# First token block in two halves, whole-row loads of q and k for two tiles, and new orders of the queues

## The chip, the cores and the metric

The kernel runs on one core of one Trainium2 chip. The metric is the device time of one execution in microseconds, median of three runs. A profile is one execution in the hardware profiler, with times counted from its first instruction. Engines are named as the profile names them: PE multiplies matrices, DVE is the vector engine, ACT the scalar engine, POOL is GpSimd, SP issues the DMAs. PEld is PE's weight load, SPq is SP's queue.

## What is computed

Chunked attention over 64 tokens at a time, then a feed-forward layer with softplus on all 4608 tokens:

```python
B, H, S, D = 8, 8, 576, 64          # chunk = 64, nc = 9
scores = scale * np.matmul(q_c, k_c.transpose(0, 1, 2, 4, 3))
scores = scores - np.max(scores, axis=-1, keepdims=True)
attn = np.exp(scores)
attn = attn / (np.sum(attn, axis=-1, keepdims=True) + 1e-09)
out = np.matmul(attn, v_c)
x = out.transpose(0, 2, 1, 3).reshape(B * S, H * D)      # 4608 x 512
h = x @ w_in                                             # w_in 512 x 2048
g = np.maximum(h, 0.0) + np.log1p(np.exp(-np.abs(h)))
return (g @ w_out).astype(np.float32)                    # w_out 2048 x 512
```

q, k and v are float32; w_in and w_out come as float64, 8 bytes a value.

## The kernel before

**Tiles and blocks.** A tile is 128 tokens (two chunks of 64), 36 in all. Four tiles are a token block m of 512 tokens, nine in all. The hidden width of 2048 is cut in 16 strips of 128. Each of the 144 pairs (m, strip), numbered g, has a first product `gemm1` (12 matmuls of 128x512 into one half of a PSUM tile `pa`), a softplus on ACT (`sp_g`, writes `u`), a split of `u` into a rounded part `g_hi` (ACT, `sp_hi`) and a rest `g_lo` (DVE or POOL, `sp_lo`), and a second product `gemm2` (12 matmuls into four PSUM tiles `po`, one a tile, over all 16 strips). Three matmuls stand for one full product, hi times lo, lo times hi and hi times hi. In PE's order G2 of pair g stands behind G1 of pair g+1: G1_0, G1_1, G2_0, G1_2, G2_1 and so on.

**Attention.** Tiles 0 to 3 go ahead of the first G1, step by step: q and k are loaded as whole rows, transposed by PE (`pe_t`), multiplied (`pe_s`), softmaxed on DVE and ACT, transposed (`pe_e`, then ACT copies), multiplied with v (`pe_v`) and split into x_hi (`att_xh`, ACT) and x_lo (`att_xl`, DVE). From tile 4 on the tiles go in pairs, as bursts of small 64x64 matmuls between the G1 and G2 of certain pairs: S of tiles 4 and 5 behind G1_3; then P V of one pair of tiles together with S of the next two, behind G1_8, behind G1_15, and behind two strips of each later block. For them `blk_load` brings q and k by 8 DMAs of 32 KB each, so placed that one DVE transpose of 128x512 by 32x32 blocks (`blk_t`) gives the operand. After the softmax DVE transposes again (`blk_e`) and 8 DMAs of 32 KB inside the chip (`blk_swap`) exchange quarters of 32 partitions.

**Weights.** 32 units (16 strips of w_in, 16 of w_out) are loaded in 512 KB DMAs (`w_load`, into a ring of three `raw` tiles) and made from float64 into a hi and a lo part: `w_top` (ACT or POOL) and `w_low` (ACT) pick pieces, `w_add` (DVE) joins them, `w_hi` and `w_lo` split the sum. Units go in the order in0, in1, out0, in2, out1, in3, ... and each must be done before its first G1 or G2; after G2_15 no weight is touched again.

**The order.** `Plan` is a list scheduler that runs when the kernel is built: each step is a task with an engine, a cost in us, the tasks it needs and an urgency; `emit` writes the steps in the order in which the plan starts them. On the chip every engine takes its instructions in that order. Tables such as `TOP_ACT`, `HI_POOL`, `LO_POOL` and `GLO_POOL` say which engine does which step. `keep_warm` writes idle matmuls of a 128x128 identity where the plan sees PE wait. All DMAs are issued by SP in one queue, 976 of them. The built program has eight DMA semaphores which take turns: a DMA waits until the one eight places ahead has landed.

Of the kernel before, what the change touches and what calls it, by code (L numbers as in the profile page):

```python
# [33 lines left out]
class Plan:  # L34
# [6 lines left out]
    FLYING = 5  # L41
# [6 lines left out]
    def add(  # L48
        self, name, eng, cost, fn, needs=(), urg=0.0, table=None, take=(), kb=0, slack=0.0, after=(), port=False
    ):  # L50
        self.tasks[name] = dict(
            name=name, eng=eng, cost=cost, fn=fn, needs=list(needs) + list(after), after=set(after), urg=urg, table=table,
            take=take, kb=kb, slack=slack, seq=len(self.tasks), port=port or eng == "POOL",
        )

    def order(self):
# [7 lines left out]
        wait, flying = {}, []  # L64
# [28 lines left out]
        while times:  # L93
# [3 lines left out]
            flying = [e for e in flying if e > now]  # L97
            for eng in list(wait):
                if free.get(eng, 0.0) > now + 1e-9 or eng == "SP" and len(flying) >= self.FLYING:
                    continue  # L100
# [17 lines left out]
                if t["kb"]:
                    dma_free = max(now + 1.8, dma_free) + t["kb"] * 1024 / self.RATE
                    end = max(dma_free + 0.8, end + 2.0)  # L120
                    flying.append(end)
# [21 lines left out]
def chunked_attention_softplus_ffn(  # L143
# [92 lines left out]
    def w_top(u):
        top = tops[u % TOP_BUFS].bitcast(F16).rearrange("p (f t) -> p f t", t=2)[:, :, 1]
# [124 lines left out]
    def pe_e(i):  # L362
        tp = ps_o.tile([P, DM], F32, name="po")
# [73 lines left out]

    def blk_swap(i):
        ea = live.pop(("eA", i))
        eT = blk_tile("eT").rearrange("p (u h k) -> p u h k", u=2, h=H)  # L440
# [5 lines left out]
        live["eT", i] = lambda r, c2, j, h2: eT[r, :, 4 * c2 + 2 * j + h2, :]  # L446
# [35 lines left out]
    def blk_v(i, pa):  # L482
        eT, vt = live.pop(("eT", i)), live.pop(("v", i))
        for j in range(2):
            for c2 in range(2):
                for h2 in range(2):
                    for a in range(2):
# [4 lines left out]
                            pa[o, a, col : col + C], vt[r, 4 * j + 2 * h2 + c2, :], eT(r, c2, j, h2),  # L492
# [79 lines left out]
    def store(m, t):  # L572
# [5 lines left out]
    T0, TG = 18.0, 5.5  # L578
    TK = (0,2)
# [33 lines left out]
    for u, (g, is_in, fc) in enumerate(units):  # L613
# [23 lines left out]
        plan.add(last[0], ph_, 0.65 if ph_ == "POOL" else 0.53, partial(w_hi, u, is_in, fc),  # L637
# [5 lines left out]
    for i in range(FIRST_BLK):  # L643
        d, kw = -60 + 3 * i, KS
        two = 2 * i // NCH != (2 * i + 1) // NCH
        for pl, (n, src) in enumerate((("q", q), ("k", k), ("v", v))):
            plan.add(f"{n}{i}", "SP", 0.6 * (1 + two), partial(pe_load, nc.sync, i, src, pl),
                     urg=VQ + i if pl == 2 else d - 6 + 0.1 * pl, kb=310,
# [145 lines left out]
```

## Time and profile before

| | us |
|---|---|
| device time, median of 3 runs | 885.03 (883.99 to 887.68) |
| the profiled execution, its own time | 883.88 |
| its span, first to last instruction | 882.0 |
| PE busy | 861.7 (98%) |
| DVE, ACT, POOL busy | 329.8, 316.8, 56.1 |
| mean granted TensorE clock | 0.998 |

The profile is read from the top down: the share of each engine, then the waits of PE, then the stretches in which they lie, and last the instructions around each wait with what released them. Matmuls of PE overlap in the records, so a group of 12 with a mean of 390 ns each takes less than 12 times that; the distance from one start to the next is what counts.

### The profile page before, as it was taken

Reading aid. Unit: us, or ns where it says so; the run is one execution under the profiler, and the core shown is the slowest. Engines: PE = TensorE matmul, PEld = TensorE weight load, DVE = VectorE, ACT = ScalarE, POOL = GpSimd, SP = SyncE. Lnnn points to the kernel's source line nnn. Section 1 sums busy time; section 2 is a strip of 40 time slices with the busy share of each in tenths; the row PEclk is TensorE's granted clock in tenths of the full one; section 3 lists DMA queues with packets and bytes.
Section 4 is the critical chain, followed back from the end, with each engine's and each line's share of the span. In section 5 each row is a group of like instructions: output and inputs, shape, how many; then the busy total and the mean of one; then the engine's idle time right before and its main releaser. Section 6 shows DMA issues by size and latency. Waiting matters only on the chain.

```text
span 882.0 us, 14812 instructions
## 1 busy us (share of the span) xinstructions
PE 861.7 (98%) x5868; PEld 700.9 (79%) x5868; DVE 329.8 (37%) x550; ACT 316.8 (36%) x494; POOL 56.1 (6%) x58
## 2 busy tenths in 40 slices
PE   8699989999999999999999999999999999999998
PEld 7577878888888888888888888888888888888886
DVE  5667854333415251524233432334153414121111
ACT  4677763232424242324232422333232423232222
POOL 1353630000000000000000000000000000000000
PEclk9999999999999999999999999999999999999999
DMA  9676763313232324132412232232223231000001
GB/s 224 171 200 201 208 149 92 62 39 63 41 86 40 63 41 100 28 64 41 105 30 46 52 62 74 41 66 42 81 39 63 44 94 31 18 18 31 1 1 48
DMA packets 214852, 63.91 MB, mean 72 GB/s; under 512 B 191744, under 2 KB 208128, under 8 KB 214784
## 3 DMA queue, kind: packets, MB, share of 16 engines
q1 hardware_dynamic: 214784, 62.98, 31.7%
q8 instruction: 46, 0.75, 0.4%
q14 instruction: 22, 0.18, 0.1%
HBM read 45.09 MB, written 9.44 MB: 62 GB/s over the span
## 4 chain that ended last, share of the span: by engine, by line
PE 87%; DMA 6%; SPq 2%; ACT 2%; POOL 1%; issue 1%; DVE 1%; DVEq 0%; ACTq 0%; POOLq 0%
PE po L560 43%; PE pa L527 41%; DMA raw<-in_moe_w_out_dram 3%; PE pa L491 2%; DMA raw<-in_moe_w_in_dram 2%; PE pa L424 2%; SPq L305 1%; DMA q<-in_q_dram 1%; ACT top L239 0%; SPq L228 0%; POOL top L239 0%; ACT low L248 0%; ACT u L538 0%; DMA k<-in_v_dram 0%; DVE low L253 0%
## 5 line engine op out<-in xcount | busy, mean ns | idle before, releaser
L538 ACT ACTIVATE u<-pa 128x512 f32<-128x512 f32 x144 | 86.0, 597 | 498.5 <-PE pa L527 498.4
L546 DVE TENSOR_TENSOR g_lo<-u,g_hi 128x512 fp32r<-128x512 f32 x136 | 94.6, 695 | 356.7 <-ACT g_hi L542 356.3
L527 PE MATMUL pa<-x,wib 128*128 128x512 f32 x864 | 208.7, 390 | 1.9 <-DVE wib L278 1.9
L527 PEld LDWEIGHTS pa<-x,wib 128*128 128x128 f32 x864 | 161.6, 188 | 38.1 <-DVE wib L278 2.3
L527 PE MATMUL pa<-x,wi_hi 128*128 128x512 f32 x576 | 178.0, 390 | 1.4 <-DVE x L507 1.4
L560 PE MATMUL po<-late,g_hi 128*128 128x512 f32 x540 | 172.1, 394 | 0.0
L527 PEld LDWEIGHTS pa<-x,wi_hi 128*128 128x128 f32 x576 | 108.1, 188 | 24.1 <-DVE x L507 1.8
L560 PEld LDWEIGHTS po<-late,g_hi 128*128 128x128 f32 x540 | 101.2, 187 | 24.4
L560 PE MATMUL po<-wo_hi,g_lo 128*128 128x512 f32 x288 | 115.6, 401 | 3.1 <-DVE g_lo L546 3.1
L560 PE MATMUL po<-late,g_lo 128*128 128x512 f32 x288 | 114.6, 398 | 0.0
L560 PE MATMUL po<-wo_lo,g_hi 128*128 128x512 f32 x288 | 114.4, 397 | 0.0
L560 PE MATMUL po<-wo_hi,g_hi 128*128 128x512 f32 x288 | 113.8, 395 | 0.0
L527 PE MATMUL pa<-x,wi_lo 128*128 128x512 f32 x288 | 112.8, 392 | 0.0
L542 ACT CAST g_hi<-u 128x512 fp32r<-128x512 f32 x144 | 89.2, 619 | 4.4
L560 PEld LDWEIGHTS po<-wo_hi,g_lo 128*128 128x128 f32 x288 | 54.4, 189 | 16.5 <-DVE g_lo L546 3.3
L527 PEld LDWEIGHTS pa<-x,wi_lo 128*128 128x128 f32 x288 | 54.0, 188 | 14.1 <-PE po L560 2.8
L560 PEld LDWEIGHTS po<-wo_hi,g_hi 128*128 128x128 f32 x288 | 54.4, 189 | 13.4
L560 PEld LDWEIGHTS po<-wo_lo,g_hi 128*128 128x128 f32 x288 | 54.4, 189 | 12.8
L560 PEld LDWEIGHTS po<-late,g_lo 128*128 128x128 f32 x288 | 54.0, 187 | 13.1
L455 DVE TENSOR_REDUCE mx<-pa 128x8 f32<-128x512 f32 x32 | 22.0, 686 | 70.0 <-ACT x L503 68.5
L412 DVE STREAM_TRANSPOSE ka<-k 128x512 f32<-128x512 f32 x30 | 21.3, 710 | 52.8 <-DMA k<-in_k_dram 42.5
L471 DVE TENSOR_REDUCE den<-qe 128x8 f32<-128x512 f32 x32 | 21.1, 660 | 16.6 <-ACT qe L466 16.6
(97 smaller groups left out, 546.0 us busy)
## 6 DMA issues: line engine op xcount, KB each, us to landing
out_dram<-raw SPq DMA_DIRECT2D x36, 256.0 KB, 2.6
raw<-in_moe_w_in_dram SPq DMA_DIRECT2D x16, 512.0 KB, 4.6
raw<-in_moe_w_out_dram SPq DMA_DIRECT2D x16, 512.0 KB, 4.5
eT<-ka SPq DMA_DIRECT2D x256, 32.0 KB, 1.9
q<-in_q_dram SPq DMA_DIRECT2D x240, 32.0 KB, 2.1
k<-in_k_dram SPq DMA_DIRECT2D x240, 32.0 KB, 2.1
q<-in_v_dram SPq DMA_DIRECT2D x60, 64.0 KB, 2.4
k<-in_v_dram SPq DMA_DIRECT2D x60, 64.0 KB, 2.4
```

The lines of the kernel that those rows point to most:

```text
L305: eng.dma_start(dst[p0 : p0 + rows], src[b, :, s0 : s0 + rows, :].rearrange("h s d -> s h d"))
L412: nc.vector.transpose(t, live.pop((n, i)))
L424: nc.tensor.matmul(pa[o, c2, col : col + C], qT[r, a * HP + hl, :], kT[r, a * HP + hl, :], start=True, stop=True,)
L455: nc.vector.tensor_reduce(mx, sc, axis=AX.X, op=ALU.max)
L471: nc.vector.tensor_reduce(den, e, axis=AX.X, op=ALU.add)
L491: nc.tensor.matmul(pa[o, a, col : col + C], vt[r, 4 * j + 2 * h2 + c2, :], eT(r, c2, j, h2), start=True, stop=True,)
L527: nc.tensor.matmul(ph, wt[:, c, fs], x[:, :, c, :], start=(n == 0), stop=(n == 3 * KC - 1))
L538: nc.scalar.activation(w["u"], w["ph"], AF.Softplus)
L542: nc.scalar.copy(w["hi"], w["u"])
L546: (nc.gpsimd if pool else nc.vector).tensor_tensor(w["lo"], w["u"], w["hi"].bitcast(F32), op=ALU.subtract)
L560: nc.tensor.matmul(pos[w["m"]][t], gg[:, ts_], wt, start=(w["first"] and n == 0), stop=(w["last"] and n == 2),)
```

## The change

It has four parts.

1. **Block 0 in halves.** `HALVES = 1`: the pair g=0 becomes two, `a0` for tiles 0 and 1 and `0` for tiles 2 and 3. Its `gemm1` makes 12 matmuls of 256 columns for each half, its softplus, hi and lo have 256 columns, its `gemm2` 6 matmuls of 512 columns for each. PE's order is G1_a0, G1_0, G2_a0, G1_1, G2_0, G1_2, ..., with the steps of tile 3's attention wherever the plan puts them.
2. **Whole rows.** Tiles 4 and 7 (`WHOLE`) load q and k by whole rows: 1 DMA of 256 KB, or 2 of 128 KB where the tile spans two batches (tile 4). `blk_t4` makes the operand by 8 DVE transposes of 32 partitions each (four for each chunk), in the place of one of 128 partitions.
3. **Tile 7's exchange.** `SWAP_DVE = (7,)`: in the place of `blk_e` and the 8 DMAs of `blk_swap`, `blk_e4` makes 8 DVE transposes of 32 partitions.
4. **Planned anew.** The planner now follows each DMA of a step by itself, with eight in flight (`FLYING = 8`); its costs, urgencies and tables have other numbers, the second burst of each later block moves from strip 13 to 14 (`BURST_AT`), and tile 2's k copy moves from DVE to ACT (`TK`). 942 DMAs are issued instead of 976.

```diff
-    FLYING = 5
+    FLYING = 8
+    AHEAD = 3.2
...
+        if i in WHOLE:
+            for p0, rows, b, s0 in rows_of(i):
+                nc.sync.dma_start(
+                    hd(dst)[p0 : p0 + rows], src[b, :, s0 : s0 + rows, :].rearrange("h s d -> s h d")
+                )
+            return
...
+    def blk_t4(i, n, c2):
+        if c2 == 0:
+            live[n + "T", i] = blk_tile({"q": "qe", "k": "ka"}[n])
+        src, dst = (t.rearrange("p (h a d) -> p h a d", h=H, a=2) for t in (live[n, i], live[n + "T", i]))
+        for tb in range(2):
+            for dh in range(2):
+                d, s = (2 * c2 + dh) * BL, (2 * c2 + tb) * BL
+                nc.vector.transpose(dst[d : d + BL, :, tb], src[s : s + BL, :, dh])
...
+    def blk_e4(i, a):
+        e = live["e", i].rearrange("p a j (u k) -> p u (a j) k", u=2)
...
+        for tb in range(2):
+            for kb in range(2):
+                d, s = (2 * a + kb) * BL, (2 * a + tb) * BL
+                nc.vector.transpose(live["eT", i][d : d + BL, tb], e[s : s + BL, kb])
...
-        ph = pa_tile()[:, 0, :MT]
+        ph = pa_tile()[:, 0, : w["cols"]]
...
-                    ph, wt[:, c, fs], x[:, :, c, :], start=(n == 0), stop=(n == 3 * KC - 1)
+                    ph, wt[:, c, fs], x[:, ts_, c, :], start=(n == 0), stop=(n == 3 * KC - 1)
...
-        for t in range(TPM):
-            ts_ = slice(t * P, (t + 1) * P)
+        for j, t in enumerate(w["tiles"]):
+            ts_ = slice(j * P, (j + 1) * P)
...
-    TOP_ACT = (0,1,4,8,9,10,11,12,13,14,15,16,18,19,23,24,26,28,29,30,31)
+    TOP_ACT = (0,3,8,9,11,15,16,17,20,21,25,26,29)
...
-    BURST_AT = (6, 13)
-    QK_AFTER = "v0"
+    BURST_AT = (6, 14)
+    QK_AFTER = "load1"
...
+    ahead = [dict(w, name=f"a{w['g']}", tiles=range(TPM // 2)) for w in blocks[:HALVES]]
+    for w in blocks[:HALVES]:
+        w["tiles"] = range(TPM // 2, TPM)
...
+            if i in SWAP_DVE:
+                plan.add(f"Tf{i}", "DVE", 1.6, partial(blk_e4, i, 0), [f"norm{i}"] + gone, urg=d)
+                plan.add(f"Te{i}", "DVE", 1.6, partial(blk_e4, i, 1), [f"Tf{i}"], urg=d)
+                swapped[i] = f"Te{i}"
...
+    for n, w in enumerate(ahead + blocks):
+        seq.append(f"G1_{w['name']}")
+        if n >= HALVES:
+            seq += [f"B{w['g']}_{j}" for j in range(2) if w["g"] in bursts]
+        if n >= LAG:
+            seq.append(f"G2_{(ahead + blocks)[n - LAG]['name']}")
```

**The start of block 0, on PE and ACT.** On PE before, the transpose of tile 3's softmax (L366), fillers (L322), its product with v (L382), fillers, and then G1_0 with 512 columns:

```order
L366 MATMUL po<-ident,x 128x128 x4
L322 MATMUL pa<-ident 128x128 x2
L382 MATMUL pa<-x,eT 64x64 x16
L322 MATMUL pa<-ident 128x128 x5
L527 MATMUL pa<-x,wi_lo 128x512
L527 MATMUL pa<-x,wi_hi 128x512 x2
```

On PE now, the last matmuls of G1_a0 (L567, 256 columns), then the same steps of tile 3 (L374, L330, L390), then the first of G1_0:

```order
L567 MATMUL pa<-x,wi_lo 128x256
L567 MATMUL pa<-x,wi_hi 128x256 x2
L374 MATMUL po<-ident,x 128x128 x4
L330 MATMUL pa<-ident 128x128 x2
L390 MATMUL pa<-x,eT 64x64 x16
L330 MATMUL pa<-ident 128x128 x6
L567 MATMUL pa<-x,wi_lo 128x256
```

The half for tiles 0 and 1 moved ahead of tile 3's last steps. On ACT before, from tile 3's x_hi (L503) to the first `g_hi` (L542); L239 is `w_top` of the unit out1, the two L248 are `w_low` of out1 and in3, L538 the load of softplus's table and the first softplus:

```order
L503 CAST x<-pa 128x512
L274 CAST wi_hi<-wib 128x4x128
L239 CAST top_98<-raw 128x512
L248 ACTIVATE wib<-raw 128x512 x2
L538 ACT_TABLE_LOAD
L538 ACTIVATE u<-pa 128x512
L274 CAST wi_hi<-wib 128x4x128
L542 CAST g_hi<-u 128x512
```

On ACT now, from `w_top` of the unit in2 (L247) to the second softplus; L256 are `w_low` of in2, out1 (x2) and in3, L542 is tile 3's x_hi:

```order
L247 CAST top_99<-raw 128x512
L578 ACT_TABLE_LOAD
L578 ACTIVATE u<-pa 128x256
L378 COPY x<-po 128x512
L582 CAST g_hi<-u 128x256
L256 ACTIVATE wib<-raw 128x512 x2
L542 CAST x<-pa 128x512
L282 CAST wi_hi<-wib 128x4x128
L256 ACTIVATE wib<-raw 128x512
L578 ACTIVATE u<-pa 128x256
```

The table load and the first softplus moved ahead of `w_low` of in2, out1 and in3; `w_low` of out1 now stands ahead of tile 3's x_hi.

**SP's queue behind the first loads.** Before, from the load of the unit in1 on; `q` and `k` are tile 4's, `x` is tile 5's q and k:

```order
L228 DMA raw<-in_moe_w_in_dram 128x4x512
L233 DMA raw<-in_moe_w_out_dram 128x2048
L404 DMA q<-in_q_dram 32x8x32 x8
L228 DMA raw<-in_moe_w_in_dram 128x4x512
L404 DMA k<-in_k_dram 32x8x32 x8
L233 DMA raw<-in_moe_w_out_dram 128x2048
L228 DMA raw<-in_moe_w_in_dram 128x4x512
L404 DMA x<-in_q_dram 32x8x32 x8
L233 DMA raw<-in_moe_w_out_dram 128x2048
L404 DMA x<-in_k_dram 32x8x32 x8
```

Now, from the same load on:

```order
L234 DMA raw<-in_moe_w_in_dram 128x4x512
L239 DMA raw<-in_moe_w_out_dram 128x2048
L234 DMA raw<-in_moe_w_in_dram 128x4x512
L408 DMA q<-in_q_dram 64x8x64 x2
L408 DMA k<-in_k_dram 64x8x64 x2
L239 DMA raw<-in_moe_w_out_dram 128x2048
L419 DMA x<-in_q_dram 32x8x32 x8
L234 DMA raw<-in_moe_w_in_dram 128x4x512
L419 DMA x<-in_k_dram 32x8x32 x8
L239 DMA raw<-in_moe_w_out_dram 128x2048
```

in2 moved ahead of tile 4's q, and tile 4's 16 issues became 4. Further on, the load of the last strip of w_in is the 136th DMA of the queue, where it was the 170th.

**DVE before the second burst.** Before, from the transpose of tile 4's softmax (L436) on; `k` is tile 6's, `x` tile 7's, L253 is `w_add`, L278 `w_lo`, L546 `g_lo`:

```order
L436 STREAM_TRANSPOSE ka<-qe 128x512
L412 STREAM_TRANSPOSE qe<-q 128x512
L436 STREAM_TRANSPOSE ka<-qe 128x512
L412 STREAM_TRANSPOSE qe<-x 128x512
L253 ISA wib<-wib,top_98 128x1024
L253 ISA wib<-wib,top_99 128x1024
L546 TENSOR_TENSOR g_lo<-u,g_hi 128x512
L278 TENSOR_TENSOR wi_lo<-wib,wi_hi 128x4x128
L253 ISA wib<-wib,top_98 128x1024
L412 STREAM_TRANSPOSE ka<-k 128x512
```

Now the last third of the stretch ahead of that burst; L426 is `blk_t`, L436 `blk_t4`:

```order
L426 STREAM_TRANSPOSE ka<-k 128x512
L436 STREAM_TRANSPOSE qe<-x 32x8x32 x4
L286 TENSOR_TENSOR wib<-low,wib 128x4x128
L261 ISA low<-low,top_98 128x1024
L261 ISA low<-low,top_99 128x1024
L286 TENSOR_TENSOR wo_lo<-low,wo_hi 128x512
L436 STREAM_TRANSPOSE ka<-x 32x8x32 x4
L586 TENSOR_TENSOR g_lo<-u,g_hi 128x512
L436 STREAM_TRANSPOSE ka<-x 32x8x32 x4
L261 ISA low<-low,top_98 128x1024
```

Tile 7's two transposes became four groups of four, spread between the weights' steps and a `g_lo`.

## Rows read from the trace of the kernel before

**Rows 1.** PE's waits: line, who released it, us in total, times, longest.

```profile
PE po L560 <- DVE g_lo L546: 3.1, 1, 3.1
PE pa L527 <- DVE wib L278: 1.9, 1, 1.9
```

**Rows 2.** Stretch: length, busy us by engine (instructions), PE clock, DMA share, GB/s.

```profile
132.00:820.00 688.00, 687.94 (x4571) 558.28 (x4570) 235.88 (x408) 219.60 (x337) 3.14 (x3) 1.00 0.26 54
```

**Rows 3.** The chain that ended last, 66 to 72 us: start, us, what.

```profile
66.29 2.79 PE po L560 x12
69.09 2.73 PE pa L527 x12
```

**Rows 4.** Timeline of PE, block 0: start, us, instruction, idle before and releaser.

```profile
31.21 0.50 PE L527 MATMUL pa<-x,wi_hi 128*128 128x512 f32 x1 [1.44 <-DVE x L507]
...
36.54 0.60 PE L322 MATMUL po<-ident 128*128 128x128 f32 x4
40.22 0.79 PE L560 MATMUL po<-wo_hi,g_lo 128*128 128x512 f32 x1 [3.08 <-DVE g_lo L546]
...
44.69 0.40 PE L527 MATMUL pa<-x,wi_lo 128*128 128x512 f32 x1
```

**Rows 5.** Timeline of ACT, 33 to 38 us.

```profile
33.04 0.78 ACT L239 CAST top<-raw 128x512 f16<-128x512 bf16 x1 [1.84 <-DMA raw<-in_moe_w_out_dram]
...
35.15 0.67 ACT L248 ACTIVATE wib<-raw 128x512 int32<-128x512 uint32 x1 [0.81 <-DMA raw<-in_moe_w_in_dram]
35.84 1.28 ACT L538 ACT_TABLE_LOAD   x1
37.13 0.60 ACT L538 ACTIVATE u<-pa 128x512 f32<-128x512 f32 x1
```

**Rows 6.** Timeline of DVE, the first lo part.

```profile
39.48 0.69 DVE L546 TENSOR_TENSOR g_lo<-u,g_hi 128x512 fp32r<-128x512 f32 x1 [0.60 <-ACT g_hi L542]
```

**Rows 7.** A stretch with its granted clock; columns as in rows 2.

```profile
41.00:42.00 1.00, 1.00 (x4) 0.80 (x3) 1.00 (x1) 0.51 (x1) 1.00 (x1) 0.50 0.46 92
```

**Rows 8.** Timeline of SP's queue: start, us of issuing, DMAs.

```profile
15.01 1.90 SPq L228 DMA_DIRECT2D raw<-in_moe_w_in_dram  x1
...
17.60 5.15 SPq L404 DMA_DIRECT2D q<-in_q_dram  x8
...
27.51 0.40 SPq L233 DMA_DIRECT2D raw<-in_moe_w_out_dram  x1
...
115.44 0.39 SPq L228 DMA_DIRECT2D raw<-in_moe_w_in_dram  x1
```

**Rows 9.** Groups of instructions: count, busy us, mean ns of one, idle before.

```profile
L412 DVE STREAM_TRANSPOSE ka<-k 128x512 f32<-128x512 f32 x30 | 21.3, 710 | 52.8 <-DMA k<-in_k_dram 42.5 <-DMA eT<-ka 10.2
...
L472 DVE TENSOR_SCALAR den<-den 128x8 f32<-128x8 f32 x36 | 7.5, 210 | 1.2
...
L334 PE MATMUL po<-ident,late 128*128 128x128 f32 x24 | 3.0, 276 | 0.0
```

**Rows 10.** Groups of instructions, PE's weight loads.

```profile
L527 PEld LDWEIGHTS pa<-x,wi_hi 128*128 128x128 f32 x576 | 108.1, 188 | 24.1 <-DVE x L507 1.8
```

**Rows 11.** Timeline of PE: bursts behind G1_3, G1_8, G1_15 and, last, an undisturbed one.

```profile
54.38 0.69 PE L424 MATMUL pa<-ka,qe 64*64 64x64 f32 x32 [0.63 <-ACT u L538]
...
82.78 0.69 PE L491 MATMUL pa<-eT,x 64*64 64x64 f32 x29
...
87.58 0.50 PE L560 MATMUL po<-wo_hi,g_lo 128*128 128x512 f32 x1
...
130.68 0.51 PE L491 MATMUL pa<-eT,k 64*64 64x64 f32 x19 [0.48 <-DMA k<-in_v_dram]
...
170.51 0.69 PE L491 MATMUL pa<-eT,q 64*64 64x64 f32 x32
...
172.56 0.50 PE L560 MATMUL po<-wo_hi,g_lo 128*128 128x512 f32 x1
```

**Rows 12.** Stretch between the first two bursts; columns as in rows 2.

```profile
60.00:85.00 25.00, 23.99 (x164) 19.39 (x162) 19.31 (x27) 18.74 (x31) 12.22 (x11) 1.00 0.69 203
```

More of the change, by code (lines that the diff above doesn't have):

```diff
@@ L48, in add @@
     def add(
-        self, name, eng, cost, fn, needs=(), urg=0.0, table=None, take=(), kb=0, slack=0.0, after=(), port=False
+        self, name, eng, cost, fn, needs=(), urg=0.0, table=None, take=(), kb=0, slack=0.0, after=(), port=False, parts=1
     ):
@@ L63, in order @@
         fin, issued, free, tab, dma_free, port = {}, {}, {}, None, 0.0, 0.0
-        wait, flying = {}, []
+        wait, landed = {}, {}
         times = [0.0]
@@ L114, in order @@
                     end = port = max(now, port) + cost
+                last = end
+                if t["kb"]:
+                    end, lanes = now, landed.setdefault(eng, [0.0] * self.FLYING)
+                    for _ in range(t["parts"]):
+                        end = max(end, lanes[-self.FLYING] + 0.1, dma_free - self.AHEAD) + cost / t["parts"]
+                        dma_free = max(end + 1.0, dma_free) + t["kb"] * 1024 / self.RATE / t["parts"]
+                        lanes.append(max(dma_free + 0.7, end + 1.8))
+                    last = lanes[-1]
                 free[eng] = end
@@ L117, in order @@
                 issued[t["name"]] = end
[L118 to L121, printed above, removed]
+                end = last
                 fin[t["name"]] = end
@@ new lines, in chunked_attention_softplus_ffn @@
+        needs += [f"xl{m * TPM + t}" for t in w["tiles"]]
+        plan.add(f"G1_{name}", "PE", 2.78 if part == 1 else 1.5, partial(gemm1, w), needs, urg=1e6, take=[("pa", [f"sp{name}"])])
+        plan.add(f"sp{name}", "ACT", 0.1 + 0.5 * part, partial(sp_g, w), [f"G1_{name}"], urg=-2, table="softplus",
+                 take=[("u", [f"lo{name}"])], after=[f"exp{FIRST_BLK - 1}"] if SP_EXP and name == "a0" else [])
+        plan.add(f"hi{name}", "ACT", 0.1 + 0.52 * part, partial(sp_hi, w), [f"sp{name}"], urg=-1, take=[("g", [f"G2_{name}"])])
@@ new lines, in chunked_attention_softplus_ffn @@
+        pool = name in GLO_POOL
+        plan.add(f"lo{name}", "POOL" if pool else "DVE", 1.3 if pool else 0.1 + 0.58 * part, partial(sp_lo, w, pool),
+                 [f"hi{name}"], urg=-1)
+        take = [("po", [f"ev{m}_{t}"]) for t in w["tiles"]] if w["first"] else []
+        plan.add(f"G2_{name}", "PE", 2.78 * part, partial(gemm2, w),
+                 [before[f"G2_{name}"], f"lo{name}", f"w_lo{of_out[fc]}", f"w_hi{of_out[fc]}"], urg=1e6, take=take,
+                 after=[f"S{FIRST_BLK - 1}"] if m == 0 and w["first"] else [])
```

143 lines of the change are left out of this document (81 added, 62 removed).

## The prediction, before the changed kernel ran

> **What bounds the kernel.** The page's busy shares say PE, 98%, but an average over the span hides where the rest lies. So the second view is PE's busy time by stretch: from 132 us to 820 us it works 687.94 of 688 us at full clock [rows 2]. Nothing on another engine can shorten that part, and the change removes no matmul from it. In the chain of work a G2 and the next G1 take 2.79 + 2.73 = 5.52 us [rows 3]; that is the dense pitch by which I measure everything ahead of 132 us. The third view is PE's own waits: the longest is the first G2 for `g_lo`, 3.1 us, another is G1_15 for a weight, 1.9 us [rows 1]. The fourth is the timeline around each wait. The time can only come from PE's holes ahead of 132 us, or be lost by new ones.
>
> Hole one is G2_0. G1_1 has issued its last matmul when the fillers start at 36.54; the first G2 starts at 40.22, 3.68 us later [rows 4]. Backwards: `g_lo` started at 39.48 [rows 6], it needed `g_hi`, which needed the softplus at 37.13; that stood behind the table load at 35.84, and this behind a weight's `w_low`, which waited for its DMA until 35.15 [rows 5]. G1_0 had finished issuing at about 33.8 (31.21 + 2.73 less one matmul), so the first softplus waited on ACT for a load it has no use for.
>
> Hole two follows from it: G2_0 takes from 40.22 to 44.69, 4.47 us [rows 4], where 2.79 is dense. [...] That is 1.68 us.
>
> Hole three is the first bursts and G1_15. The burst behind G1_8 takes from 82.78 to 87.58, 4.80 us, where an undisturbed one takes 172.56 - 170.51 = 2.05: 2.75 us lost. The bursts behind G1_3 and G1_15 lost 0.63 and 0.48 [rows 11], G1_15 the 1.9. Together 5.76 us.
>
> **The change, part by part.**
>
> *Halves.* x_lo of tile 3 ended G1_0's wait at 31.21 [rows 4]. The half a0 needs tiles 0 and 1 only, so its matmuls lie ahead of tile 3's last steps, in PE time that was idle or filler. What then remains of G1 0 is half of it, 2.73/2 = 1.37 us less. A matmul of 256 columns is in no row. The nearest are 128x128 transposes, 24 in 3.0 us or 0.125 us each [rows 9], the weight load, 0.188 us [rows 10], and half of the dense 0.2275, 0.114. I take 0.13 (the weight changes with each matmul, as in the transposes): 12 x 0.13 = 1.6 us, 0.23 over the half; bounds 1.37 and 2.26 us. [...] G2 makes the same 12 matmuls in two halves: nothing. Net gain 1.37 - 0.23 = 1.14 us, if the remaining half can start no later than before.
>
> *Can it?* x_hi of tile 3 now stands on ACT behind `w_low` of out1. Before, out1's issue came at 27.51, because tile 4's q held the queue for 5.15 us from 17.60 and its k followed; it landed at 33.04 [rows 5, 8]. Now in2 and four issues lie between: five times about 0.6 us, so the queue is free near 20.6. But out1 also needs in1's `raw` buffer: in1, issued at 15.01, lands near 21 and `w_top` takes 0.78. So the issue comes at about 21.8, 5.7 us earlier, the landing at 33.04 - 5.7 = 27.3 or, as it now follows 1 MB closely, 28.7. Then `w_low` 0.67, x_hi 0.6, a `w_add` 0.65 and x_lo 0.68 on DVE (partly side by side): G1_0's half starts near 31.0. I count no gain and no loss here; bounds -1 (tile 3's own chain) and +4 us (out1 as late as before).
>
> *Softplus.* The table load now follows `w_top` of in2, which lands near 24.5 instead of 27, since it is issued where q was, at 17.60. Table 1.28 and softplus follow G1_a0, and `g_lo` of a0 is there about 2 us ahead of G2_a0, which follows G1_0 at once. `g_lo` of the second half has G2_a0 and the whole G1_1 to hide in, 1.4 + 2.73 us, against a chain of 0.35 + 0.35 + 0.4 plus a wait for in3's `w_low`, some 2 us. So hole one closes, 3.68 us (bounds 0 and 3.68). With no stretch of 3 us without work ahead of the first G2, hole two closes too: 1.68 us. The cover would be gone if in3 lands over 2 us later than I think.
>
> *The queue of loads.* 34 DMAs fewer are issued, and the last strip of w_in is the 136th instead of the 170th. Between 27.51 (the 33rd) and 115.44 (the 170th) one issue took (115.44 - 27.51)/137 = 0.64 us [rows 8]. The last strip so comes about 34 x 0.64 = 22 us earlier by count; in part the queue will wait for buffers and for the swaps of tiles 4 and 5, which must follow their softmax, so I take 13. The demand comes 8 to 9 us earlier (3.68 + 1.68 + 1.14 = 6.5 from the start, the rest from the first bursts). G1_15's 1.9 us and the 0.48 go. The burst behind G1_8 needs the last DMA of v of tile 5, now 27 places earlier (17 us), but those DMAs follow the swap of tile 5, which moves with the first burst, 6.5 us. I leave it 1.2 us of its 2.75, the first burst 0.3, and 0.5 for waits that I don't see: 5.76 - 2.0 = 3.8 us gained; bounds 5.8 (none left) and -3.
>
> *DVE transposes.* Tiles 4 and 7 trade five transposes of 0.71 us [rows 9] for 40 of 32 partitions and 256 elements each. No row has one. A 128x8 operation takes 0.21 and the 128x512 transpose 0.71 [rows 9]; between them by elements, 0.45. So 40 x 0.45 - 3.6 = 14 us more DVE work. Between 60 and 85 us DVE is busy 19.31 of 25 us [rows 12], and tile 7's 16 lie in that stretch: 16 x 0.45 - 1.4 = 5.8 us. It becomes full and just not late; queued behind them are `g_lo` and `w_add`, and PE waits for those. Bounds: 0.21 and 0.71 each. [...] Hidden, I count nothing.
>
> *The rest.* The later bursts move one strip back; in rows 2 they cost no wait, and three products lie between x_lo and its first use. POOL gets more weight steps; its 12.22 of 25 us [rows 12] has room. Moving tile 2's copy to ACT: inside the lead.
>
> **Sum.** 3.68 + 1.68 + 1.14 + 3.8 = 10.3 us. The profiled execution took 883.88, so 873.6; the median lies 1.15 above that execution, so 874.7.
>
> **Rivals.**
> *A, out1 late.* If it lands near 33 as before, x_lo of tile 3 comes at 35 and G1_0's half with it: 4 us back, about 879. For it: 1 MB in flight ahead of it. Against: the queue ahead of it is 7 us shorter (10 less 3).
> *B, DVE full.* At 0.71 us a piece, tile 7's 16 take 4 us more, and the burst behind G1_8 or a `g_lo` waits: about 879.
> *C, the loads set the pace.* The holes at 82 and 125 us show weights and v arriving just when PE wants them. If they come no earlier, PE starts 6.5 us earlier only to wait: 883, no change. Against: 34 issues fewer.
> *D, slower.* A small transpose costs over twice a whole one, as its source and target partitions differ and no row shows that. Tile 7's q and k are needed behind G1_8, where my walk leaves 3 us to spare: 16 x (t - 0.45) - 3 exceeds the gain of 10.3 from t = 1.28 us on, and 10.3 + 4.4 (0.5% slower) from 1.56 on; at 1.8 it gives 893. Against: 0.71 for twice the elements.
>
> **Chances.** Forecast 0.62, A 0.12, B 0.12, C 0.09, D 0.05. Within 0.5% (about what a measurement here can tell from no change) is 880.6 to 889.5. A and B lie below it: faster 0.85, same 0.10, slower 0.05. The range takes the forecast's bounds and A and B: low 870 (no later wait, tile 3 one microsecond earlier), high 881.
>
> **What would show it.** PE's waits should no longer list the first G2 for `g_lo`; the clock should stay at 1.00 from 30 to 50 us; G1_2 should start near 38.2 instead of 44.69; `w_low` of out1 on ACT should end its wait near 29; the 32-partition transposes should take about 0.45 us, the 256-column matmuls 0.13 in pitch. I am wrong if ACT waits for a load between G1_a0 and the first `g_hi`, if PE waits for `g_lo` or tile 7's operands near 76 us, or if PE's holes ahead of 132 us stay near 13 us in all.

## The result, and the profile after

The changed kernel takes 878.05 us (median of 4, 877.37 to 878.49); the kernel before 886.22 beside it. The ratio is 0.9909, 95% interval 0.9884 to 0.9935: faster by 0.9%, as predicted, but by less than predicted (874.7 was 10.3 us under the 885.03 of before). The profiled execution took 878.49 us with a span of 876.7, against 883.88 and 882.0: these 5.3 us of span are what the traces can explain. The medians lie 8.2 us apart. The profiled execution of before lies below the four timed ones (883.99 to 887.68), and the longer executions of that kernel have a lower mean granted clock (beside e9 and e10 a span of 886.6 us at 0.990, 881.4 at 0.998); no profile shows where they lose it, so the other 3 us stay open. Of all executions behind this text one, of e3, was slow (1423.12 us at a granted clock of 0.557) and is left out of e3's median and ratio. From 132 to 820 us PE works 687.94 us in both [rows 2], so the gain lies ahead of 132 us. In starts (us) read from PE's timelines:

| | G1_2 | G1_4 | G1_9 | G2 behind the burst of G1_15 | span |
|---|---|---|---|---|---|
| before | 44.69 | 57.88 | 90.48 | 131.65 | 882.0 |
| after | 43.12 | 55.94 | 88.06 | 126.32 | 876.7 |
| gained | 1.57 | 1.94 | 2.42 | 5.33 | 5.3 |

So the later holes gave 5.3 - 1.57 = 3.7 us, where the sum had 3.8. The head gave 1.57 instead of 6.5. PE's waits of after (columns as in rows 1); the first G2 and G1_15 are gone from the list, the wait for `x_lo` of tile 3 (1.44 before, rows 4) is now the longest, and v is waited for behind G1_8:

```profile
PE pa L567 <- DVE x L546: 2.1, 1, 2.1
PE po L374 <- DVE late L517: 2.1, 3, 1.2
...
PE pa L530 <- DMA x<-in_v_dram: 1.2, 2, 0.6
```

PE's timeline of after, against rows 4 and 11:

```profile
32.18 0.39 PE L567 MATMUL pa<-x,wi_lo 128*128 128x256 f32 x1 [0.27 <-ACT x L542]
34.67 0.67 PE L567 MATMUL pa<-x,wi_hi 128*128 128x256 f32 x2 [2.10 <-DVE x L546]
...
37.06 0.63 PE L600 MATMUL po<-wo_hi,g_lo 128*128 128x512 f32 x1
...
43.12 0.40 PE L567 MATMUL pa<-x,wi_lo 128*128 128x512 f32 x1
...
84.20 0.51 PE L530 MATMUL pa<-eT,x 64*64 64x64 f32 x19 [0.59 <-DMA x<-in_v_dram]
...
85.17 0.50 PE L600 MATMUL po<-wo_hi,g_lo 128*128 128x512 f32 x1
```

The half of G1_0 starts at 32.18, stops after one matmul for `x_lo` of tile 3 and goes on at 34.67; I had said 31.0. From there to G1_1 at 38.99 it takes 4.32 us for 11 matmuls of 256 columns (1.3 at the pitch below) and half a G2 (1.40). The stretches (columns as in rows 2) show why: the granted clock is at 0.50 again from 36 to 38 us, as it was in hole two (rows 7), and costs 1.6 us (4.32 less 1.3 and 1.40), as before.

```profile
34.00:36.00 2.00, 1.33 (x7) 1.33 (x8) 1.99 (x5) 0.00 (x0) 0.61 (x1) 0.71 1.04 276
36.00:38.00 2.00, 2.00 (x9) 1.81 (x9) 1.93 (x5) 1.35 (x3) 0.77 (x1) 0.50 0.50 76
```

VectorE's timeline says what `x_lo` stood behind:

```profile
27.18 1.29 DVE L261 CUSTOM_DVE_ANT_0 wib<-wib,top 128x1024 uint16<-128x1024 uint16 x1
...
29.00 1.77 DVE L436 STREAM_TRANSPOSE qe<-q 32x256 f32<-32x256 f32 x4
30.80 0.43 DVE L586 TENSOR_TENSOR g_lo<-u,g_hi 128x256 fp32r<-128x256 f32 x1
31.14 2.88 DVE L261 CUSTOM_DVE_ANT_0 wib<-wib,top 128x1024 uint16<-128x1024 uint16 x2
33.94 0.68 DVE L546 TENSOR_TENSOR x<-pa,x 128x512 fp32r<-128x512 f32 x1
```

Its `x_hi` ended on ACT at 32.13, but VectorE's queue held two `w_add`s until 33.94. The engine had no room: from 24 to 50 us VectorE was busy 14.45 of 26 us in the kernel before (first line) and 25.36 in the changed one (second):

```profile
24.00:50.00 26.00, 20.05 (x147) 16.21 (x147) 14.45 (x23) 15.81 (x26) 9.62 (x10) 0.93 0.76 186
```

```profile
24.00:50.00 26.00, 21.41 (x162) 18.07 (x163) 25.36 (x44) 15.78 (x28) 13.13 (x14) 0.93 0.75 184
```

And there is a view of before that I had read only for its pitch [rows 3]: the chain that ended last, here from 16 to 56 us: its shares and three of its pieces (start, us, what).

```profile
by line: DMA raw<-in_moe_w_in_dram 39.4%; DMA raw<-in_moe_w_out_dram 21.5%; DMA q<-in_q_dram 12.4%; POOL top L239 5.4%; SPq L228 4.8%; ACT top L239 3.9%; PE po L560 2.8%; issue 2.7%; DVE wib L253 2.2%; PE pa L424 1.7%; ACT u L538 1.5%; ACT 
...
28.02 7.11 DMA raw<-in_moe_w_in_dram
...
46.37 4.51 DMA raw<-in_moe_w_in_dram
...
53.73 0.60 ACT u L538
```

It runs through the loads to the softplus ahead of the first burst, and not through holes one and two at all. In the changed kernel the same view from 23 to 36 us runs through VectorE (first line: `w_add`, the small transposes, `x_lo`):

```profile
by line: DVE wib L261 35.9%; DVE qe L436 12.7%; issue 12.7%; PE pa L567 11.7%; DVE x L546 10.3%; DVE mx L494 5.3%; DVE den L510 4.7%; DVE wi_lo L286 4.6%; DVE g_lo L586 3.3%; DVE den L512 1.6%; DVE den L511 1.4%; DVE x L499 0.3%
```

### The profile page after: what moved, and what is told of

It reads as the page before. It is cut to its first block, busy times and chain, and to the rows that moved or that the text cites. A ratio compares the mean times of both kernels' runs of the same rounds, so it can differ in the third digit from the quotient of the medians.

```text
span 876.7 us, 14820 instructions
## 1 busy us (share of the span) xinstructions
PE 861.6 (98%) x5874; PEld 701.5 (80%) x5874; DVE 348.5 (40%) x589; ACT 309.4 (35%) x483; POOL 65.3 (7%) x68
## 4 chain that ended last, share of the span: by engine, by line
PE 89%; DMA 4%; DVE 4%; SPq 1%; issue 1%; ACT 1%; POOL 0%; DVEq 0%; POOLq 0%; ACTq 0%
PE po L600 42%; PE pa L567 41%; PE pa L530 2%; DMA raw<-in_moe_w_in_dram 2%; PE pa L449 2%; DMA raw<-in_moe_w_out_dram 1%; PE po L330 1%; DVE wib L261 1%; SPq L322 1%; DVE mx L494 0%; DVE den L510 0%; DMA q<-in_q_dram 0%; DMA x<-in_v_dram 0%; DVE g_lo L586 0%; DVE x L546 0%
## 5 line engine op out<-in xcount | busy, mean ns | idle before, releaser
L578 ACT ACTIVATE u<-pa 128x512 f32<-128x512 f32 (+1 forms) x145 | 86.2, 594 | 510.1 <-PE pa L567 505.4
L586 DVE TENSOR_TENSOR g_lo<-u,g_hi 128x512 fp32r<-128x512 f32 (+1 forms) x137 | 94.9, 693 | 295.3 <-ACT g_hi L582 295.0
L567 PE MATMUL pa<-x,wib 128*128 128x512 f32 x864 | 208.6, 390 | 0.0
L567 PEld LDWEIGHTS pa<-x,wib 128*128 128x128 f32 x864 | 161.7, 188 | 36.0 <-PE po L600 2.4
L567 PE MATMUL pa<-x,wi_hi 128*128 128x512 f32 (+1 forms) x584 | 179.3, 389 | 2.1 <-DVE x L546 2.1
L567 PEld LDWEIGHTS pa<-x,wi_hi 128*128 128x128 f32 x584 | 109.9, 189 | 24.3 <-DVE x L546 2.3
L567 PE MATMUL pa<-x,wi_lo 128*128 128x512 f32 (+1 forms) x292 | 114.0, 390 | 1.3 <-POOL top L247 1.0
L582 ACT CAST g_hi<-u 128x512 fp32r<-128x512 f32 (+1 forms) x145 | 89.4, 616 | 4.4
L567 PEld LDWEIGHTS pa<-x,wi_lo 128*128 128x128 f32 x292 | 55.2, 189 | 15.7 <-PE po L600 2.9
L426 DVE STREAM_TRANSPOSE qe<-q 128x512 f32<-128x512 f32 x29 | 20.5, 707 | 65.5 <-DMA k<-in_k_dram 46.3
L426 DVE STREAM_TRANSPOSE ka<-k 128x512 f32<-128x512 f32 x29 | 20.6, 711 | 51.1 <-DMA k<-in_k_dram 33.8
```

Source lines behind the costliest of these rows:

```text
L567: nc.tensor.matmul(ph, wt[:, c, fs], x[:, ts_, c, :], start=(n == 0), stop=(n == 3 * KC - 1))
L578: nc.scalar.activation(w["u"], w["ph"], AF.Softplus)
L582: nc.scalar.copy(w["hi"], w["u"])
L586: (nc.gpsimd if pool else nc.vector).tensor_tensor(w["lo"], w["u"], w["hi"].bitcast(F32), op=ALU.subtract)
```

## Experiments

Theory: at the head the order in VectorE's and ACT's queues decides. Rival, C of the prediction: the loads set the pace, and what the head gains is given back. All starts in us from PE's timelines, spans of the profiled executions; the ratio is to the kernel before beside them. e8 is the changed kernel once more.

| | G1_2 | G1_4 | G1_9 | span | median | ratio (95%) |
|---|---|---|---|---|---|---|
| e8, the changed kernel again | 43.06 | 55.70 | 86.55 | 875.1 | 877.00 | 0.9918 (0.9901 to 0.9934) |
| e1 | 39.67 | 54.09 | 85.12 | 873.9 | 876.10 | 0.9921 (0.9899 to 0.9942) |
| e5 | 38.17 | 54.08 | 85.01 | 873.7 | 875.97 | 0.9907 (0.9893 to 0.9922) |
| e6 | 38.88 | 54.71 | 86.10 | 874.8 | 876.70 | 0.9915 (0.9900 to 0.9929) |
| e10 | 38.25 | 52.65 | 84.94 | 874.8 | 877.55 | 0.9909 (0.9884 to 0.9934) |
| e11 | 41.89 | 54.54 | 85.97 | 874.5 | 876.85 | 0.9913 (0.9882 to 0.9944) |
| e12 | 37.59 | 52.27 | 85.34 | 874.0 | 876.36 | 0.9912 (0.9883 to 0.9941) |
| e2 | 44.48 | 57.08 | 87.55 | 881.1 | 880.80 | 0.9959 (0.9945 to 0.9973) |
| e3 | 39.60 | 53.58 | 93.54 | 887.3 | 885.94 | 1.0012 (0.9996 to 1.0029) |
| e4 | 43.33 | 55.96 | 94.12 | 891.6 | 892.38 | 1.0096 (1.0078 to 1.0114) |
| e7 | 46.15 | 58.86 | 90.85 | 882.9 | 884.25 | 0.9992 (0.9983 to 1.0001) |
| e9 | 41.60 | 59.47 | 91.79 | 884.9 | 886.71 | 1.0015 (0.9999 to 1.0031) |

The scatter from one execution to the next is to be seen between the changed kernel (G1_2 43.12, G1_9 88.06, span 876.7) and e8 (43.06, 86.55, 875.1). The profiled executions of e2 and e3 are the longest of their runs (882.92 and 889.12 us, 2 to 3 above the medians), so their starts and spans overstate a loss by up to that much.

> The changed kernel itself, for a comparison on the same chip: 876.5 to 879 us, span 876 to 878, G1_2 at 43.1, the waits of x_lo of tile 3 (2.1 us) and of v behind G1_8 (1.2 us) as before, if they are not chance.

The wait for `x_lo` came again (1.93 us). The wait for v behind G1_8 did not (0.2 us instead of 1.2), so its size is in part chance.

**e1, the order alone.** Two steps move forward in the planner's list: `x_hi` of tile 3 in front of `w_low` of out1, `x_lo` of tile 3 in front of the two `w_add`s.

```diff
+    MOVES = [('xh3', 'w_low4'), ('xl3', 'w_add3')]
...
-        last = 0.0
-        for start, t in self.order()[0]:
+        last, out = 0.0, self.order()[0]
+        for name, front in self.MOVES:
+            t = next(t for t in out if t[1]["name"] == name)
+            out.remove(t)
+            out.insert([u[1]["name"] for u in out].index(front), t)
...
+        for start, t in out:
```

> Only the order of four instructions is new: on ACT x_hi of tile 3 goes ahead of w_low of out1, on VectorE x_lo of tile 3 goes ahead of the two w_adds (of in2 and out1) that took 31.14 to 33.94 us in the changed kernel. Theory (x_lo of tile 3 was late because of what stood ahead of it on VectorE and ACT, and PE's stop then cost the clock): x_hi follows V3 at about 30.5, x_lo starts at 31.2 to 31.7 instead of 33.94, the half of G1_0 runs without the wait of 2.1 us, the granted clock stays 1.00 from 32 to 40 us, G1_1 starts near 35 instead of 38.99. The second G2 then waits for its g_lo, since that softplus stands behind w_low of in3 (landed 36.48): G1_2 starts at 40 to 41 instead of 43.12, a gain of 2 to 3 us at the head, and 875 to 876 us in all if the later holes stay. Rival C (loads set the pace): the head gains the same, but the waits behind G1_8 and later grow by as much, 878. Rival A (the landing of out1 decides): x_lo comes no earlier than 33, no gain, 878.

`x_lo` started at 30.36, its wait went, and from 32 to 46 us the clock stayed at 1.00 (first line; from 20 to 40 us its mean in e1 was 0.91, with two waits of 0.9 and 0.8 us ahead of the half a0). The other two lines show the next waits:

```profile
36.00:38.00 2.00, 1.09 (x5) 0.56 (x3) 1.94 (x5) 0.50 (x2) 0.15 (x1) 1.00 0.76 123
```

```profile
38.18 0.50 PE L610 MATMUL po<-wo_hi,g_lo 128*128 128x512 f32 x1 [1.08 <-DVE g_lo L596]
44.12 0.47 PE L610 MATMUL po<-wo_hi,g_lo 128*128 128x512 f32 x1 [1.54 <-DVE g_lo L596]
```

G1_2 came 3.4 us earlier; half of that is left at G1_4 (1.6 to 1.9), 1.4 to 2.9 at G1_9. So the order made the wait of 2.1 us and the clock of 0.50 behind it. That is shown. The next waits, for two `g_lo`s (above), are of the same kind: the first of them holds up the G2 of the half 0, which in the changed kernel did not wait, as the stop for `x_lo` had given its softplus time.

**e5, the same for the softplus.** `MOVES` goes on:

```diff
+    ("sp0", "w_lo4"), ("hi0", "w_lo4"), ("lo0", "w_lo4"), ("hi1", "Tk4"), ("lo1", "Tk4"),
```

> The order of e1_xlo_first with five more instructions moved: the softplus and g_hi of the half block go ahead of w_low of in3 on ACT, g_hi of block 1 ahead of w_low of out2, and on VectorE g_lo of the half goes ahead of w_lo of out1 and g_lo of block 1 ahead of the second half of tile 4's k transposes. Theory (ACT and VectorE queues order the head): the waits of the second G2 (1.08 us) and the third (1.54 us) that e1 showed go, G1_2 starts near 38.4 (39.67 in e1, 43.12 in the changed kernel), G1_3 at 44 to 44.7 (46.99 in e1); the burst behind G1_8 then waits 0 to 1.5 us longer than in e1, since the last v is issued by the same queue: span 871.5 to 873.5, time 873 to 875. Rival C (loads set the pace, the whole gain is given back behind G1_8): span 873.9 as in e1, burst behind G1_8 2.5 us longer.

The head gained 1.5 us over e1, and at G1_4 nothing of it is left (54.08 and 54.09). PE now stopped behind G1_3 and ahead of G1_4 (first two lines). The rest are pieces of the chain that ended last, from 36 us on:

```profile
49.41 0.69 PE L449 MATMUL pa<-ka,qe 64*64 64x64 f32 x32 [1.63 <-ACT u L578]
54.08 0.47 PE L567 MATMUL pa<-x,wi_lo 128*128 128x512 f32 x1 [0.97 <-DVE qe L499]
```

```profile
36.10 0.44 DVE qe L436
...
45.01 1.40 DVE wib L261
...
48.62 4.24 DMA raw<-in_moe_w_in_dram
```

The place of the wait moved, its size stayed (1.08 and 1.54 in e1, 1.63 and 0.97 here). That is the rival's result, and its span (873.7), but not its way: the burst behind G1_8 took 3.0 us, no longer than in e1, and the chain runs through VectorE from 24 to 46 us, with its first load at 48.62.

**e6 and e10, v from another queue, and more moves.** In e6 the eight DMAs of v of tiles 4 and 5 go out from GpSimd, between 66 and 74 us. In e10 six more steps move.

```diff
-                nc.sync.dma_start(
+                (nc.gpsimd if i in V_POOL else nc.sync).dma_start(
+    ("v4", "load17"), ("v5", "load18"),                                              # e6 and e10
+    ("sp3", "w_low9"), ("hi3", "w_low9"), ("sub4", "lo3"), ("sub5", "lo3"),          # e10
+    ("sp8", "w_low18"), ("hi8", "w_low18"),                                          # e10
```

> As e5_softplus_first, and the eight DMAs of v of tiles 4 and 5 are issued by GpSimd between its own instructions (about 62 to 73 us) instead of SP's queue, where they took 5.3 us. Theory (what paces the stretch of 55 to 125 us is the time of issues in the one queue): v lands before the burst behind G1_8, which takes 2.1 to 2.4 us instead of 3.3, every later load is issued about 5 us earlier: span 1.2 to 2.5 us under e5. Rival (the DMA engines' bandwidth is the limit): v lands no earlier, span as e5. [...]

> As e6_v_on_pool, with four more moves of the same kind: softplus and g_hi of block 3 ahead of the w_lows of in5 and out4, softplus and g_hi of block 8 ahead of the w_lows of out8 and in10, and VectorE's subtractions of tiles 4 and 5 ahead of g_lo of block 3. Theory (a softplus that waits behind a load's w_low in ACT's queue is what gave the gain of e5 and e6 back, 1.6 us behind G1_3, 1.0 at G1_4, 0.6 to 1.0 behind G1_8): these waits go, G1_4 starts at 52 to 53 (54.08 in e5), the burst behind G1_8 takes 2.1 to 2.5 us (3.1 in e5 and e6): span 871 to 873, time 872.5 to 874.5. Rival C (the loads set the pace; each wait removed comes back at the next weight): G1_9 at 85 to 86 as in e5 and e6, span 873.5 to 875, the wait now on a w_lo or w_hi.

GpSimd issued four v DMAs in 2.62 us (e6, timeline of POOL), as fast as SP (eight in 5.32 us in the changed kernel), and PE no longer waited for v. It waited for the softplus that reads the PSUM buffer instead (first fence, e6), and where e10 moved that too, for `x_lo` (second fence, e10). G1_9 came no earlier than in e5, and so both theories failed: in e6 the last load of w_in was issued at 108.10 (106.74 in e5) although the queue had eight issues fewer, and in e10 G1_4 (52.65) and the burst (2.4 us) came as expected, the span (874.8) did not. Rival C's span came, but PE's new waits are for `x_lo` and a `g_lo`, not for a weight, and e10's chain meets no load between 22 and 95 us.

```profile
66.77 2.62 POOL L322 DMA_DIRECT2D x<-in_v_dram  x4
...
81.50 0.84 PE L530 MATMUL pa<-eT,x 64*64 64x64 f32 x29 [0.61 <-ACT u L578]
```

```profile
84.94 2.99 PE L567 MATMUL pa<-x,wib 128*128 128x512 f32 x12 [0.80 <-DVE x L546]
```

**e11 and e12, VectorE's work taken away.** One 128x512 transpose in place of eight small ones, in the order of the changed kernel (e11) and of e5 (e12). It leaves the quarters where they are, so these two kernels serve for the time alone.

```diff
-                nc.vector.transpose(dst[d : d + BL, :, tb], src[s : s + BL, :, dh])   # 8 times
+            nc.vector.transpose(live[n + "T", i], live[n, i])                          # once
```

> The changed kernel with the q and the k of tiles 4 and 7 transposed by one 128x512 transpose each (0.71 us) instead of eight small ones (8 x 0.44 us); the quarters then stay where they are, so the attention of these two tiles is not the reference's. All else, loads and order, is as in the changed kernel: VectorE has 4 x (3.55 - 0.71) = 11.4 us less to do, half of it between 29 and 43 us, half between 62 and 81. Theory 1 (VectorE, full from 24 to 50 us, holds x_lo, w_add and w_lo back): x_lo of tile 3 starts about 1 us earlier than 33.94, G1_2 near 41.5 to 42.3 (43.1), G1_4 near 53.5 (55.7 to 55.9), span 872 to 874.5 against 875.1 and 876.7. Theory 2 (loads alone set the pace): the head moves up to 1 us, G1_9 within 0.7 us of the changed kernel's 86.6 to 88.1, span 875 to 876.5.

> The same shortened transposes (tiles 4 and 7 not the reference's) in the order of e5_softplus_first. Theory 1 (VectorE): VectorE's busy time from 24 to 50 us falls from 25.6 of 26 us to 20 to 22, the waits behind G1_3 (1.6 us) and at G1_4 (1.0 us) shrink by half or more, G1_4 at 51 to 53 (54.08 in e5), G1_9 at 82 to 84 (85.01), span 870 to 872.5 (873.7). Theory 2 (loads): VectorE's queue empties but PE waits for the same weights: G1_4 at 53.5 or later, G1_9 at 84.5 or later, span 873 to 874.

In e12 VectorE is busy 21.70 of 26 us, the head is the earliest of all, G1_4 1.8 us ahead of e5; G1_9 is not (85.34). The chain from 24 to 52 us is now one of loads, as in the kernel before, and behind G1_8 PE waits for v:

```profile
24.00:50.00 26.00, 23.37 (x207) 19.36 (x208) 21.70 (x32) 17.32 (x30) 16.50 (x18) 1.00 0.78 186
```

```profile
by line: DMA raw<-in_moe_w_out_dram 41.8%; DMA raw<-in_moe_w_in_dram 32.8%; POOL top L247 7.1%; DVE g_lo L586 6.2%; DVE mx L494 4.3%; DVE wib L261 3.7%; ACT wib L256 2.4%; DVE qe L499 2.1%; issue 1.5%; SPq L239 0.4%; POOLq L247 0.1%; SPq L2
...
81.49 0.51 PE L530 MATMUL pa<-eT,x 64*64 64x64 f32 x19 [0.94 <-DMA x<-in_v_dram]
```

In e11 the head gains 1.2 us on e8, the span 0.6. So the small transposes cost the head up to 1.8 us, as theory 1 had it (G1_4 at 52.27 in e12, G1_2 at 41.89 in e11), and the end nothing that can be measured here (medians of 876.85 and 876.36, e8 877.00, e5 875.97), as theory 2 had it.

**e3 and e4, one tile of the loads edit undone.**

```diff
-    WHOLE = (4,7)
+    WHOLE = (7,)              # e3; e4: WHOLE = (4,), SWAP_DVE = ()
```

> WHOLE = (7,): tile 4 is loaded by quarters again (16 issues instead of 4) and transposed by two 128x512 transposes; tile 7 as in the changed kernel. VectorE has 16 x 0.44 - 2 x 0.71 = 5.6 us less to do between 28 and 43 us, the queue 12 issues of about 0.6 us more. Theory (VectorE is full at the head): VectorE's busy share from 24 to 50 us falls from 25.4 of 26 to about 21, x_lo of tile 3 starts 1 to 2 us earlier, G1_2 at 41 to 42; but every load behind it comes some 5 to 7 us later, so PE waits 3 to 6 us more between 60 and 132: 879 to 882. Rival C alone (queue decides all): the head does not gain, 882 to 885. Rival B alone (VectorE decides all): 875.

> WHOLE = (4,), SWAP_DVE = (): tile 7 is loaded by quarters, transposed by whole transposes and exchanged by eight DMAs again; tile 4 as in the changed kernel. 20 issues more (about 12 us of queue), 24 x 0.44 - 3 x 0.71 = 8.4 us less VectorE work between 60 and 100 us. Theory (queue): the head is the same (G1_2 at 43.1), the last load of w_in is issued 5 to 12 us later than 110.19, the bursts behind G1_8 and G1_15 or G1_15 itself wait 3 to 6 us more: 881 to 884. Rival B (VectorE was the limit there): 876 to 877.

In e3 VectorE is free (18.03 of 26 us) and the head 3.5 us earlier without any move; from there to G1_9 it takes 53.9 us instead of 44.9, with 12 more issues in SP's queue; 4.3 us of that are PE's waits for the low parts of two weights. In e4 the queue (first fence) begins v at 82.71 (76.48 in the changed kernel), and PE stands behind G1_8 (second):

```profile
59.44 4.65 SPq L419 DMA_DIRECT2D x<-in_q_dram  x8
64.20 0.39 SPq L234 DMA_DIRECT2D raw<-in_moe_w_in_dram  x1
64.63 4.66 SPq L419 DMA_DIRECT2D x<-in_k_dram  x8
...
82.71 5.30 SPq L322 DMA_DIRECT2D x<-in_v_dram  x8
```

```profile
86.64 1.64 PE L530 MATMUL pa<-eT,x 64*64 64x64 f32 x29 [5.33 <-DMA x<-in_v_dram]
```

Both are dearer than I expected (879 to 882 and 881 to 884). Undoing either loses the whole gain; the planner wrote the order anew with tables made for both, so the share of the loads alone is not shown.

**e7 and e9, the loads edit alone, in the order of before.** e7 is the kernel before with `WHOLE = (4, 7)` and `SWAP_DVE = (7,)`, no halves, its own order; e9 moves tile 4's transposes behind the first two `g_lo`s.

```diff
+MOVES = [("Tq4", "q6"), ("Tk4", "w_lo6")]   # e9
```

> The kernel before in its own order, with one edit only: tiles 4 and 7 are loaded in whole rows and transposed in 32-partition pieces, tile 7's softmax output is exchanged by VectorE (34 DMAs fewer, 14 us more of VectorE work); no halves, no new plan. Theory (issues in the queue are the pace): out1 lands some 5 us earlier, so the first softplus no longer waits for its w_low until 35.15 and hole one shrinks without any halves; G1_2 starts at 40.5 to 43 instead of 44.69, the burst behind G1_8 loses 1 us instead of 2.75, G1_15 no longer waits: 875 to 879. Rival B (the small transposes fill VectorE): the bursts or g_lo wait, 882 to 886. Rival (only the new plan makes the edit useful): within 1 us of before.

> As e7_before_whole (the kernel before, whole rows for tiles 4 and 7, no halves, no new plan), but VectorE's two groups of eight small transposes of tile 4 (3.59 us each), which stood ahead of x_lo of tiles 2 and 3 there, come behind the first and the second g_lo. Theory (in e7 the gain of the freer queue was eaten by VectorE, which has no room ahead of block 0): x_lo of tile 3 starts 4 to 5 us earlier than its 34.43, the whole G1_0 continues at 29.5 to 31 instead of 34.4, the first softplus no longer waits for a load (w_low of out1 and of in3 are landed by 33), G1_2 starts at 39 to 41.5 instead of 46.15 (44.69 in the kernel before); the later waits grow in part, since w_add and the loads are no earlier: 878 to 881. Rival (the loads set the pace, whatever the head does): G1_2 as above, but 883 to 885. Rival (the lead of e7 was long for another reason): x_lo of tile 3 not before 33, 884.

e7 is no faster than before. Two blocks of eight transposes stand ahead of `x_lo` (VectorE's timeline of e7), the whole G1_0 begins at 33.38 instead of 29.29, and the mean granted clock from 24 to 50 us is 0.74 (0.93 in the kernel before):

```profile
24.66 3.59 DVE L427 STREAM_TRANSPOSE qe<-q 32x256 f32<-32x256 f32 x8 [0.27 <-DMA q<-in_q_dram]
...
30.21 3.58 DVE L427 STREAM_TRANSPOSE ka<-k 32x256 f32<-32x256 f32 x8
...
34.43 0.68 DVE L536 TENSOR_TENSOR x<-pa,x 128x512 fp32r<-128x512 f32 x1
```

e9 puts that right (G1_2 at 41.60) and loses it at the first burst, where PE waits 3.8 us for a softplus: it stands in ACT's queue behind a `w_hi` that itself waits 1.72 us for a `w_add`. With 886.71 us it came out above all that I expected. So 34 issues fewer bring nothing in the order of before, with the transposes early or late; of the orders tried only the new one turned them into a gain. At hole one they do work without halves: the first G2 no longer waits in e7 and waits 0.8 us in e9, where it was 3.08.

**e2, halving undone.** `HALVES = 0`.

> HALVES = 0: block 0 is one block of 512 tokens again, everything else as in the changed kernel (the planner then puts the first softplus behind w_low of out1 and of in3, as one softplus follows the whole G1_0). Theory: hole one is back, the first G2 waits for g_lo behind a load, about 2 us or more, the clock falls to 0.5 behind it, and G1_2 starts at 44.5 to 46 instead of 43.12: 880 to 882 us. Rival (halving brought nothing, as x_lo of tile 3 and its wait took its place): G1_2 within 0.5 us of 43.12, 878.

Hole one is back: the first G2 waits 2.04 us for `g_lo`, the clock is at 0.56 to 0.59 from 40 to 44 us, G1_2 starts at 44.48. The median is 3.8 us above e8. In the profiled execution, which is 2.1 us above that median, 1.4 us lie at the head and 1.0 is left at G1_9; the larger part lies behind G1_9, around G1_12, where PE waits for a weight's low part (2.0 us), in an order that the planner wrote anew. Halving is worth 1.4 us at the head; how much of the 3.8 is its own stays open.

## Why the prediction was right, and where it failed

- *Right: the sign, and the later holes.* G1_15 does not wait, its burst lost 0.4 us (5.14 less 2.73 and 2.05), the burst behind G1_8 2.1 where I left it 1.2. That 3.7 us came for 3.8 is in part luck: by the table 2.9 us lie between G1_9 and the burst of G1_15, where I had 2.4, and only 0.5 between G1_4 and G1_9, where I had 1.55. I had taken 0.48 for the burst of G1_15, its last wait alone; by its length before (below, from its first product to the G2 behind it, less 2.05) it lost 1.0. Nor was my reason right in full: the last load of w_in is issued at 110.19, 5.3 us before its 115.44, and not 13.

```profile
128.62 0.69 PE L491 MATMUL pa<-eT,q 64*64 64x64 f32 x32
...
131.65 0.50 PE L560 MATMUL po<-late,g_lo 128*128 128x512 f32 x1
```

- *Right, with luck: holes one and two.* The G2 of the half 0 does not wait. But the stop for `x_lo` gave its softplus, behind in3's `w_low` on ACT, time to finish; with the stop gone (e1) that G2 waits 1.08 us and the next 1.54. The cover that I counted, 1.4 + 2.73 us, was too short.
- *Right: the unit prices.* A small transpose takes 0.44 us (0.45 taken). The 256-column matmuls have a pitch of 0.119 (0.13 taken), from the ninth start behind the first pair of the half a0:

```profile
26.01 0.40 PE L567 MATMUL pa<-x,wi_hi 128*128 128x256 f32 x2
...
27.08 0.40 PE L567 MATMUL pa<-x,wi_hi 128*128 128x256 f32 x2
```

- *Wrong: "Can it?".* I had the half start near 31.0, behind `x_lo` of tile 3; this ended at 34.62 and the half went on at 34.67. out1 was issued at 23.87 instead of 21.8 and its `w_low` ended its wait at 30.97 instead of 29 (rival A in part), but in e1 `x_lo` starts at 30.36, ahead of that `w_low`'s result. What I left out was VectorE's queue ahead of 50 us: I counted one `w_add` of 0.65 us ahead of `x_lo`, and two stood there with 2.88. I looked for a full VectorE between 60 and 85 us [rows 12] and never asked for the same row at 24 to 50, where 16 small transposes and earlier `w_add`s came to lie. With the stop of 2.1 us (I had named a stretch of 3) the clock was at 0.50 again, and a wait of 2.1 and a clock loss of 1.6 took the place of holes one and two (5.36 us).
- *Wrong: the sum.* I added holes as if each microsecond at the head reached the end. e5 against e8 gains 4.9 at G1_2, 1.6 at G1_4, 1.5 at G1_9 and 1.4 in the span, and the last two are no more than the scatter between the changed kernel and e8 (1.5 and 1.6). Rival C had the result right for the head: what was gained there was given back. Its reason, that the loads set the pace, is seen in the chain of before, through loads from 17 to 54 us, and in e12; in e5 and e10 the chain runs through VectorE, so that reason is not shown for the head in general. For the later holes C failed: they closed, with the loads issued 5.3 us earlier, and waits for weights and v came back where e3 and e4 put issues back.
- *Open.* What keeps G1_9 at 85 to 86: with VectorE eased PE waits for v (e12), with v from another queue it waits for ACT and VectorE (e6, e10). Two chains of nearly one length would look so; both cures in one kernel were not tried, so this is argued and not shown. e1 and e5 have the lowest medians, but their intervals overlap those of the changed kernel.

## What to carry to other kernels

Before adding up PE's holes, follow the chain that ended last across them: a hole that is not on it gives back only what the chain leaves. When work moves to an engine, ask for its busy time in the stretch where the work will stand in the queue, not over the span. In an in-order queue look at what is ahead of the step PE waits for; moving that step forward cost nothing here, but each cure showed the next wait.

## Unexpected on the hardware

A `w_add` on VectorE took 0.65 to 0.69 us where GpSimd was idle (mean 0.68 of 13 in the changed kernel), and 0.90 to 1.65, mean 1.17, where GpSimd was busy for over nine tenths of it (6 of them). Between these the share does not fix the price: the 1.29 at 27.18 above had GpSimd busy for 0.58 of it, the second of the two at 31.14 took 1.76 at 0.68, and two others took 0.68 at 0.79. Small transposes took 0.44 and 0.43 in the two cases. A `w_add` reads two tiles, a transpose one; what makes the difference is not shown. The planner counts 0.68 for a `w_add` and lets it wait for GpSimd (`port=True`). For `w_lo`, which reads two tiles too, it makes no such allowance: on VectorE it took 0.68 with GpSimd idle (mean of 7) and 0.86 to 1.83 with GpSimd busy for over nine tenths of it (4).
